# Block 0's routing moved into block 3's slots, with attention, table and load steps of a fused SSM and two-MoE kernel respaced

## The chip, the cores and the metric

One core of one Trainium2 chip runs the whole program. The metric is the device time of one execution in microseconds (us). The core has five engines with instruction queues of their own: TensorE (PE in the profile, with PEld for its weight loads), VectorE (DVE), ScalarE (ACT), GpSimd (POOL) and SyncE (SP, which here mainly issues DMA transfers). Each queue runs in order; engines wait for one another by semaphores.

## The reference

The program computes three layers one after the other.

```python
# 1: decayed linear attention: batch 4, heads 8, 768 steps, head size 32, state 16
y[:, :, sl] = einsum(C B * L, x) + einsum(C, state) * exp(cum)   # chunk by chunk, state carried on
x = y.transpose(0, 2, 1, 3).reshape(3072, 256)
# 2: an MoE layer without routing (leaky ReLU with a slope of its own for each feature)
h = x @ w_in                       # 256 -> 2048
x = (max(h, 0) + alpha * min(h, 0)) @ w_out     # 2048 -> 256
# 3: top-1 routing over 8 experts
logits = x @ w_gate + modality_bias[modality_id]
e = argmax(logits); gate = softmax(logits)[e]
out = gate * (max(x @ w1[e], 0) @ w2[e])        # 256 -> 1024 -> 256
```

## The kernel before

**Tiling.** The 3072 tokens are 24 chunks of 128. Chunks form nine blocks: blocks 0, 1 and 2 have two chunks, blocks 3 to 8 have three. A block goes through attention (`attn_*`, or `at_scan`, `at_mt`, `attn_c`, `attn_d` in the later part), then through layer 2 in 16 units of 128 features (`unit_mm` makes `ph`, `unit_act` and `unit_split` make `g`, `gh`, `gl`, `unit_g2` adds the second product into `px`), then through routing. Products are done in split precision: a high and a low part of each operand, three matmuls for one product.

**Two schedules.** Blocks 0 to 2 with the first attention stand in a part whose instruction order a scheduler chooses. From block 3 on the order is written by hand: a list of *slots*, 16 for each of the blocks 3 to 8 (slots 0 to 95, counted here from block 3's first unit), then 8 for each of 14 *items* (slots 96 to 207). An item is a page of up to 256 tokens of one expert in layer 3. A slot issues its unit's first product and activation, the split of the unit before, the second product of the unit four slots back (`LAG` is 4), and then whatever stands in the list `todo` for that slot, in the order in which the `do(...)` calls were made. Each engine runs its share of this in that order.

**Routing of a block k** (`route_at`): `route_mm` and `route_act` for each of its chunks (product `pxr`, logits `L`, and the copy of the tokens into the tile `xr` by ACT, line 499), `route_b` (which expert), `route_exp`, `route_gate` (the gate), `route_c` (product `pr`, counts in front of each token), `route_d` (row numbers `pi`), `route_out` (one indirect DMA by POOL per chunk, which scatters the rows of `xr` into the sorted DRAM array `srt`, line 573). For block 0 all of that stands ahead of the slots.

**Item tables.** When enough blocks have been counted, `item_tables` works out which expert and which page an item has: table 0 (items 0 and 1), table 1 (items 2 to 8), table 2 (the rest). It is a generator; each `yield` ends the step done in one slot. SP reads a table entry, then issues `item_load` (four transfers of 512 KB) and `item_rows` (258 KB out of `srt`). Each item's weights are split into high and low parts by ACT and DVE (`item_split`), its rows transposed (`item_tr_mm` on PE, `item_tr_act` on ACT and DVE, which give `x2h` and `x2l`). `tail_counts` writes zeros behind the last rows of every expert (eight writes of 645 KB).

**Shared buffers.** `ph`, and for blocks 0 to 2 `pxr` and `pr`, share three PSUM buffers (tag `h`). The attention's `ps` and `py` share two (tag `s`). `xr` has two SBUF buffers for all blocks in turn (`tag="xr"`, `bufs=2`), `xT` has one. `split_part` turns the attention's B and C into three bf16 parts each for chunks 17 to 23.

```python
    do(u, split_load, g)
    for q in range(6):
        do(v + q, split_part, g, q % 2, q // 2)
```

Of the kernel before, what the change touches and what calls it, by code (L numbers as in the profile page):

```python
# [35 lines left out]
NFULL = 12  # L36
# [76 lines left out]
def ssm_moe_moe_kernel(  # L113
# [25 lines left out]
    NS = 3  # L139
    blocks = [(sum(SIZES[:k]), n) for k, n in enumerate(SIZES)]  # L140
# [333 lines left out]
    def route_a(k, ts=None):  # L474

        n = blocks[k][1]
        for t in range(n) if ts is None else ts:
            route_mm(k, t)
            route_act(k, t)

    def route_mm(k, t):
        if t == 0:
            blk[k]["xr"] = work.tile([P, MX, ROW], F32, tag="xr", name="xr", bufs=2)
            blk[k]["L"] = small.tile([P, MX, NE], F32, tag="L", name="L")
        p = route_ps(k, [P, 512], "pxr", t)
        ts_ = slice(t * P, (t + 1) * P)
        pk = p[:, :KD * (P + NE)].rearrange("p (k w) -> p k w", k=KD)
        for kk in range(KD):
            mm(pk[:, kk], blk[k]["xT"][:, kk, ts_], idwg[:, kk], True, True)
        blk[k]["pk"] = pk  # L490
# [58 lines left out]
    def wait_for(i, o, why):  # L549
        tc.add_manual_dep(i, o.name, mybir.DependencyInfo(mybir.DependencyClass.Sync, mybir.DependencyReason.DATA),  # L550
                          reason=why)
# [18 lines left out]
    def route_out(k, ts):  # L570
        pi, xr = blk[k]["pi"], blk[k]["xr"]
        for t in ts:
            sc = nc.gpsimd.indirect_dma_start(
                out=srt[:, :], out_offset=bass.IndirectOffsetOnAxis(ap=pi[:, t:t + 1].bitcast(U32), axis=0),
                in_=xr[:, t, :ROW], in_offset=None, bounds_check=NROW - 1, oob_is_err=False)

            for o in scat + (tails if k < len(blocks) - 1 else []):
                tc.declare_no_dep(sc.ins, o, reason="rows are disjoint")
            scat.append(sc.ins)
            if k == len(blocks) - 1:  # L580
                for o in tails:
                    wait_for(sc.ins, o, "rows behind the last ones")
# [105 lines left out]
    def item_tables(j, pool):  # L688

        V = nc.vector
        use = cst[:, C_USE:C_E]
        u3 = use.rearrange("p (e j) -> p e j", j=NSL)
        cb = cnt[:, :, None].to_broadcast([P, NE, NSL])

        def compare(o, d, op):
            V.scalar_tensor_tensor(o.rearrange("p (e j) -> p e j", j=NSL), cb, d, u3, ALU.add, op)

        rk = pool.tile([P, 3, NS_], F32, tag="rk", name="rk", bufs=1)  # L700
        if j == 0:
            compare(sets[:, 0], -float(PG), ALU.is_ge)
            lo, hi, base = 0, 1, 0.0
        elif j == 1:
            compare(sets[:, 1], -float(PG), ALU.is_ge)
            compare(sets[:, 2], 0.0, ALU.is_gt)
            V.tensor_tensor(sets[:, 2], sets[:, 2], sets[:, 1], ALU.subtract)
            V.tensor_tensor(sets[:, 1], sets[:, 1], sets[:, 0], ALU.subtract)
            lo, hi, base = 0, 3, 0.0
        else:  # L710
            compare(sets[:, 0], -float(P), ALU.is_gt)
            compare(sets[:, 1], 0.0, ALU.is_gt)
            V.tensor_tensor(sets[:, 1], sets[:, 1], sets[:, 0], ALU.subtract)
            V.tensor_tensor(sets[:, :2], sets[:, :2], knw[:, None, :].to_broadcast([P, 2, NS_]), ALU.mult)
            lo, hi, base = 0, 2, float(N_KNOWN)
        w = hi - lo
        sf = sets[:, lo:hi].rearrange("p s n -> p (s n)")
        rf = rk[:, :w].rearrange("p s n -> p (s n)")
        V.tensor_tensor_scan(rf, cst[:, C_ONE:C_ONE + 1].to_broadcast([P, w * NS_]), sf, base, ALU.mult, ALU.add)
        yield  # L720
        if j == 2:

            nd = small.tile([P, 2], F32, tag="nd", name="nd", bufs=1)
            V.tensor_scalar(nd[:, 0:1], rk[:, 0, NS_ - 1:], float(-NFULL), 0.0, ALU.add, ALU.max)
            V.tensor_scalar(nd[:, 1:2], rk[:, 1, NS_ - 1:], float(-NSTATIC), 0.0, ALU.add, ALU.max)
            V.tensor_tensor(tbli, nd[:, 0:1], nd[:, 1:2], ALU.max)
            yield
        V.tensor_tensor(rf, rf, sf, ALU.mult)
        r1 = rk[:, 0]
        for s in range(1, w):  # L730
            V.tensor_tensor(r1, r1, rk[:, s], ALU.add)
        yield
        if j == 1:

            V.tensor_scalar(knw, r1, float(N_KNOWN), None, ALU.is_gt)
            nz = rk[:, 1]
            V.tensor_scalar(nz, r1, 0.0, None, ALU.is_equal)
            V.tensor_tensor(knw, knw, nz, ALU.add)
            yield
        va = pool.tile([P, 2, NS_], F32, tag="va", name="va", bufs=1)  # L740
        V.scalar_tensor_tensor(va, r1[:, None, :].to_broadcast([P, 2, NS_]), cst[:, C_IT:C_IT + 1],
                               cst[:, C_USE:C_IT].rearrange("p (r n) -> p r n", r=2), ALU.is_equal, ALU.mult)
        tf = small.tile([P, 2], F32, tag="tf", name="tf", bufs=1)
        V.tensor_reduce(tf, va, AX.X, ALU.add)
        V.tensor_copy(tab[j], tf)
        yield
# [169 lines left out]
    for u, (k, fc) in enumerate(early):  # L916
# [3 lines left out]
        if k == 0:  # L920
            g = fc // 2
# [17 lines left out]
        if side is not None:  # L939
# [5 lines left out]
            if left <= 0 or u + 1 == end:  # L945
# [1 line left out]
                    pass  # L947
                side = None
                nk += 1
    for step in (route_a, route_b, route_exp, route_gate, route_c, route_d):  # L950
        step(0)
    route_out(0, range(blocks[0][1]))

    last = len(blocks) - 1
    slots = [("m",) + q for q in late] + [("i", i, fc) for i in range(NSTATIC) for fc in range(KF2)]
    at = {q[1:]: u for u, q in reversed(list(enumerate(slots))) if q[0] == "m"}
# [4 lines left out]
    def do(u, fn, *args):  # L963
        todo.setdefault(u, []).append((fn, args))
# [65 lines left out]
    def route_at(k, mms, b):  # L1030
        for t, u in enumerate(mms):
            do(u, route_mm, k, t)
            do(u + 1, route_act, k, t)
        for v, fn in zip(b, (route_b, route_exp, route_gate, route_c, route_d)):
            do(v, fn, k)

        n = blocks[k][1]
        if k < last:
            for t in range(n):
                do(b[-1] + 1 + t, route_out, k, (t,))  # L1040
        else:
            do(b[-1], route_out, k, range(n))

    u = at[NS, 0]
    route_at(1, (u, u + 1), (u + 4, u + 5, u + 6, u + 7, u + 9))
    route_at(2, (u + 5, u + 7), (u + 9, u + 10, u + 11, u + 12, u + 15))
    for k in range(NS, last + 1):
        u = at[k, 15] + 1
        if k < last - 1:
# [4 lines left out]
    def table_at(u, j, pool):  # L1054
        steps = []

        def step():
            if not steps:
                steps.append(item_tables(j, pool[-1]))
            next(steps[0], None)  # L1060

        for v in range(u, u + 5):
            do(v, step)

    table_at(at[last - 1, 14], 0, small_)
    table_at(at[last, 13], 1, m2p)
    do(at[last, 11], tail_counts)
    table_at(ui + 12, 2, m2p)

    for k in range(NS, last):  # L1070
        c0, n = blocks[k + 1]
        if k == NS:
            do(at[k, 0], load_next, c0 + 1)
            do(at[k, 0], prep_dec, k + 1, 0)
        for j in range(n):
            c, b = c0 + j, at[k, 0] + 5 * j - (k > NS)
            for h in range(2):
                do(b + h, at_scan, c, h)
            do(b + 2, at_mt, c, k + 1, j)
            do(b + 2, load_next, c + 2)  # L1080
            if j + 1 < n:
                do(b + 3, prep_dec, k + 1, j + 1)
            do(b + 4, attn_c, c, k + 1, j)
            do(b + 5, attn_d, c, k + 1, j)
        if k + 2 <= last:
            do(at[k, 9], load_block, k + 2)
            do(at[k, 15], prep_dec, k + 2, 0)
    for g, u, v in ((1, at[NS, 8], at[NS + 1, 1]),):
        do(u, split_load, g)
        for q in range(6):  # L1090
            do(v + q, split_part, g, q % 2, q // 2)
    do(at[NS, 15], new_pools)
    do(at[last - 1, 15], end_attention)

# [1 line left out]
    do(at[last, 3], item_rows, 0)  # L1096
    do(at[last, 4], lambda: item_load(1))
    do(at[last, 4], item_rows, 1)
    do(at[last, 13], item_tr_mm, 0)
    do(at[last, 14], item_tr_act, 0)  # L1100
    do(ui + 2, item_tr_mm, 1)
    do(ui + 3, item_tr_act, 1)
    for q in range(8):
# [1 line left out]
        do(at[last, 15] + q, item_split, 1, q // 2, (q % 2,))  # L1105
    for i in range(2, NSTATIC):
        b = ui + KF2 * (i - 2)
        do(b, item_load, i, 1 if i >= NFULL else 2)
        do(b if i == 2 else b + 6, item_rows, i)
        b += KF2  # L1110
        for q in range(8):
            do(b + q, item_split, i, q // 2, (q % 2,))
        do(b + 4, item_tr_mm, i)
        do(b + 5, item_tr_act, i)

# [101 lines left out]
```

## Time and profile before

| | us |
|---|---|
| median of 3 runs | 583.43 |
| lowest and highest | 581.81, 584.33 |
| the profiled execution | 582.98 |
| its span, first to last instruction | 581.2 |
| TensorE busy in the span | 552.0 |
| DVE, ACT, POOL busy | 434.1, 315.0, 238.9 |

The span is 1.8 us shorter than that execution's own time, which also holds what lies before the first and behind the last instruction. Slot 0 begins at 145.7 us in the profile, slot 16 (block 4) at 192.6, slot 96 (item 0) at 401.3; the last product ends near 567.

### The profile page before, as it was taken

What the parts mean: (1) busy time and instruction counts of PE and PEld (TensorE: products, weight loads), DVE (VectorE), ACT (ScalarE), POOL (GpSimd) and SP (SyncE); (2) the same over time, 40 slices, a digit from 0 to 9 for tenths busy, and PEclk for the clock granted to TensorE, in tenths of its full rate; (3) what the DMA queues carried; (4) which work ended last, traced back from release to release, by engine and by line L of the source; (5) the groups of instructions that cost most, each with busy time, mean ns of one, the idle gap of its engine ahead of it and who ended that gap; (6) DMA issues with size and microseconds to landing.
All of it is one profiled execution on the core that took longest, in us unless ns stands there. A gap on an engine that the chain in (4) does not pass through costs nothing. (4 is left out here: it accounts for less than half of the span.)

```text
span 581.2 us, 12122 instructions
## 1 busy us (share of the span) xinstructions
PE 552.0 (95%) x4303; PEld 516.9 (89%) x4303; DVE 434.1 (75%) x857; ACT 315.0 (54%) x696; POOL 238.9 (41%) x258
## 2 busy tenths in 40 slices
PE   8989989998999989999999999997999999999993
PEld 7867878898989779999998999997999999999993
DVE  4999999834677777777767776579688778777860
ACT  0446657756434464444443444575567776677761
POOL 1144345655445645654754844746022122111211
PEclk9795999999799999999999999999999999999998
DMA  7956654420037245234234210468969867776400
GB/s 240 296 179 199 191 186 130 148 77 12 19 109 209 81 131 173 88 107 150 68 114 147 79 46 2 146 210 226 284 227 327 254 212 225 235 240 202 152 17 6
DMA packets 59123, 89.27 MB, mean 154 GB/s; under 512 B 5070, under 2 KB 37008, under 8 KB 59056
## 3 DMA queue, kind: packets, MB, share of 16 engines
q1 hardware_dynamic: 55942, 80.73, 44.7%
q0 software_dynamic: 2400, 6.32, 3.0%
q10 hardware_dynamic: 714, 1.38, 0.8%
q8 instruction: 36, 0.59, 0.4%
q14 instruction: 31, 0.25, 0.1%
HBM read 73.50 MB, written 15.17 MB: 153 GB/s over the span
## 5 line engine op out<-in xcount | busy, mean ns | idle before, releaser
L622 POOL TENSOR_TENSOR gl<-g,gh 128x384 fp32r<-128x384 f32 (+1 forms) x144 | 143.0, 994 | 147.6 <-ACT gh L620 147.1
L611 ACT ACTIVATE t<-ph,sgn 128x384 f32<-128x384 f32 (+1 forms) x144 | 78.6, 546 | 121.8 <-PE ph L153 115.2
L613 DVE SCALAR_TENSOR_TENSOR g<-ph,sal,t 128x384 f32<-128x384 f32 (+1 forms) x144 | 81.2, 565 | 76.4 <-ACT t L611 69.7
L153 PE MATMUL ph<-xh,wi_h 128*128 128x384 f32 (+1 forms) x288 | 99.3, 347 | 2.7 <-DVE g L613 2.4
L153 PE MATMUL px<-gl,wo_h 128*128 128x384 f32 (+1 forms) x288 | 94.2, 327 | 2.3 <-POOL gl L622 2.2
L153 PE MATMUL px<-gh,wo_h 128*128 128x384 f32 (+1 forms) x288 | 93.7, 326 | 0.2 <-ACT xT L650 0.2
L153 PE MATMUL ph<-xl,wi_h 128*128 128x384 f32 (+1 forms) x288 | 92.8, 323 | 1.1 <-DVE xl L159 1.1
L153 PE MATMUL px<-gh,wo_l 128*128 128x384 f32 (+1 forms) x288 | 93.3, 324 | 0.4 <-DVE wo_l L159 0.4
L153 PE MATMUL ph<-xh,wi_l 128*128 128x384 f32 (+1 forms) x288 | 92.8, 323 | 0.0
L620 ACT CAST gh<-g 128x384 fp32r<-128x384 f32 (+1 forms) x144 | 67.6, 470 | 17.1 <-DVE g L613 16.5
L880 POOL DMA_INDIRECT out_dram<-ob,xr x26 | 29.3, 1126 | 112.0 <-ACT ob L879 55.4
L857 ACT ACTIVATE rh<-ph 128x256 fp32r<-128x256 f32 (+1 forms) x112 | 41.6, 371 | 53.0 <-PE ph L153 51.4
L153 PEld LDWEIGHTS ph<-xh,wi_h 128*128 128x128 f32 x288 | 55.1, 192 | 7.9 <-DVE g L613 3.9
L858 DVE SCALAR_TENSOR_TENSOR rl<-ph,rh 128x256 fp32r<-128x256 f32 (+1 forms) x112 | 45.1, 402 | 21.4 <-ACT rh L857 20.4
L153 PEld LDWEIGHTS px<-gl,wo_h 128*128 128x128 f32 x288 | 55.7, 193 | 4.0 <-POOL gl L622 2.7
L153 PEld LDWEIGHTS ph<-xl,wi_h 128*128 128x128 f32 x288 | 55.3, 192 | 1.6 <-DVE xl L159 1.4
L153 PEld LDWEIGHTS px<-gh,wo_h 128*128 128x128 f32 x288 | 55.8, 194 | 1.0 <-ACT xT L650 0.5
L153 PEld LDWEIGHTS px<-gh,wo_l 128*128 128x128 f32 x288 | 55.8, 194 | 0.8 <-DVE wo_l L159 0.6
L153 PEld LDWEIGHTS ph<-xh,wi_l 128*128 128x128 f32 x288 | 55.3, 192 | 0.2 <-issue 0.2
L969 DVE TENSOR_TENSOR_SCAN ab<-ab,id 128x512 f32<-128x512 f32 x30 | 44.0, 1468 | 0.0
L153 PE MATMUL ph<-x2h,wi_h 128*128 128x256 f32 x144 | 41.3, 286 | 0.0
L153 PE MATMUL ph<-x2l,wi_h 128*128 128x256 f32 x144 | 40.4, 280 | 0.0
(149 smaller groups left out, 1291.0 us busy)
## 6 DMA issues: line engine op xcount, KB each, us to landing
raw<-in_w_dram SPq DMA_DIRECT2D x56, 512.0 KB
ab<-a_scr SPq DMA_DIRECT2D x24, 512.0 KB
srt<-zr SPq DMA_DIRECT2D x8, 645.0 KB
raw<-in_w_in_dram SPq DMA_DIRECT2D x8, 512.0 KB
raw<-in_w_out_dram SPq DMA_DIRECT2D x8, 512.0 KB
xr<-srt SPq DMA_DIRECT2D x14, 258.0 KB
bs<-bcs SPq DMA_DIRECT2D x30, 96.0 KB
bs<-bcs SPq DMA_DIRECT2D x15, 192.0 KB
```

Source lines behind the costliest of these rows:

```text
L153: nc.tensor.matmul(o, l, r, start=start, stop=stop)
L611: nc.scalar.activation(t[:, :N], ph[:, :N], AF.Copy, scale=sg)
L613: nc.vector.scalar_tensor_tensor(g[:, :N], ph[:, :N], sal[:, fc:fc + 1], t[:, :N], ALU.mult, ALU.max)
L620: nc.scalar.copy(gh[:, :N], g[:, :N])
L622: nc.gpsimd.tensor_tensor(gl[:, :N], g[:, :N], f(gh[:, :N]), ALU.subtract)
L857: nc.scalar.activation(rh[:, :n], ph[:, :n], AF.Relu)
L858: nc.vector.scalar_tensor_tensor(rl[:, :n], ph[:, :n], 0.0, f(rh[:, :n]), ALU.max, ALU.subtract)
L880: nc.gpsimd.indirect_dma_start(out=out[:, :], out_offset=bass.IndirectOffsetOnAxis(ap=xr[:, t, ROW - 1:ROW].bitcast(U32), axis=0), in_=ob, ...
L969: nc.vector.tensor_tensor_scan(lt[:, s_].rearrange("p h i -> p (h i)"), lt[:, s_].rearrange("p h i -> p (h i)"), id8[:, s_].rearrange("p h ...
```

## The change

- Ahead of the slots only `route_a(0)` is left. Block 0's `route_b`, `route_exp`, `route_gate`, `route_c`, `route_d` go to slots 0 to 4, its two scatters to slots 5 and 6.
- Block 2's `route_d` goes from slot 15 to slot 13, its scatters from 16 and 17 to 14 and 15.
- In block 3's slots the attention of chunks 10 and 11 begins one slot sooner (slots 4 and 9).
- The six `split_part` steps stand in every second slot (17, 19, ... 27) and no more in six slots running.
- Table 1 has two more steps, so that its last one is in slot 98 and no more in 96; item 2's load, and with it its rows and its splits, come two slots later (98 and 106 to 113). Item 0's transposes come one slot sooner (92, 93) and are registered ahead of the table's steps.

```diff
         elif j == 1:
             compare(sets[:, 1], -float(PG), ALU.is_ge)
             compare(sets[:, 2], 0.0, ALU.is_gt)
+            yield
             V.tensor_tensor(sets[:, 2], sets[:, 2], sets[:, 1], ALU.subtract)
             V.tensor_tensor(sets[:, 1], sets[:, 1], sets[:, 0], ALU.subtract)
             lo, hi, base = 0, 3, 0.0
...
+        if j == 1:
+            yield
         w = hi - lo
...
-    for step in (route_a, route_b, route_exp, route_gate, route_c, route_d):
-        step(0)
-    route_out(0, range(blocks[0][1]))
+    route_a(0)
...
     u = at[NS, 0]
+    route_at(0, (), (u, u + 1, u + 2, u + 3, u + 4))
     route_at(1, (u, u + 1), (u + 4, u + 5, u + 6, u + 7, u + 9))
-    route_at(2, (u + 5, u + 7), (u + 9, u + 10, u + 11, u + 12, u + 15))
+    route_at(2, (u + 5, u + 7), (u + 9, u + 10, u + 11, u + 12, u + 13))
...
-        for v in range(u, u + 5):
+        for v in range(u, u + 7):
             do(v, step)
 
+    do(at[last, 12], item_tr_mm, 0)
+    do(at[last, 13], item_tr_act, 0)
     table_at(at[last - 1, 14], 0, small_)
     table_at(at[last, 13], 1, m2p)
...
-            c, b = c0 + j, at[k, 0] + 5 * j - (k > NS)
+            c, b = c0 + j, at[k, 0] + 5 * j - (k > NS or j > 0)
...
-            do(v + q, split_part, g, q % 2, q // 2)
+            do(v + 2 * q, split_part, g, q % 2, q // 2)
...
-    do(at[last, 13], item_tr_mm, 0)
-    do(at[last, 14], item_tr_act, 0)
...
-        do(b, item_load, i, 1 if i >= NFULL else 2)
-        do(b if i == 2 else b + 6, item_rows, i)
+
+        w = 2 if i == 2 else 0
+        do(b + w, item_load, i, 1 if i >= NFULL else 2)
+        do(b + w if i == 2 else b + 6, item_rows, i)
         b += KF2
         for q in range(8):
-            do(b + q, item_split, i, q // 2, (q % 2,))
+            do(b + w + q, item_split, i, q // 2, (q % 2,))
```

## Rows read from the trace of the kernel before

**Rows 1.** The page's first part: busy time, share of the span, instructions.

```profile
PE 552.0 (95%) x4303; PEld 516.9 (89%) x4303; DVE 434.1 (75%) x857; ACT 315.0 (54%) x696; POOL 238.9 (41%) x258
```

**Rows 2.** Stages: length, busy us (instructions) by engine, granted clock, DMA share, GB/s.

```profile
143.40:161.70 18.30, 15.64 (x105) 14.49 (x104) 12.73 (x38) 7.52 (x19) 8.38 (x10) 0.81 0.13 41
...
405.80:409.30 3.50, 3.50 (x16) 3.50 (x15) 3.40 (x8) 1.34 (x4) 1.01 (x1) 0.52 1.09 271
412.30:430.00 17.70, 17.32 (x151) 17.08 (x150) 12.50 (x41) 11.39 (x28) 1.00 (x1) 1.00 1.02 303
432.50:567.00 134.50, 134.45 (x1145) 134.25 (x1144) 104.87 (x206) 94.22 (x218) 27.33 (x25) 1.00 0.65 203
```

**Rows 3.** TensorE's timeline, slots 0 to 5: start, us, line, [idle before <-releaser].

```profile
142.28 1.09 PE L153 MATMUL pxr<-idwg,xT 128*128 128x136 f32 x8
...
145.55 0.17 PE L153 MATMUL pr<-oh,tri 128*128 128x8 bf16 x1 [2.18 <-DVE oh L519]
...
146.73 0.52 PE L153 MATMUL ph<-xh,wi_l 128*128 128x384 f32 x1
...
153.39 0.28 PE L153 MATMUL px<-gh,wo_l 128*128 128x256 f32 x1
...
161.75 0.45 PE L153 MATMUL ph<-xh,wi_h 128*128 128x384 f32 x1
...
164.41 0.39 PE L153 MATMUL ps<-bs 128*128 128x128 bf16 x4
```

**Rows 4.** TensorE's timeline in block 4's slots: rows with a wait.

```profile
194.16 0.44 PE L153 MATMUL ph<-xl,wi_h 128*128 128x384 f32 x1 [1.13 <-DVE xl L159]
...
213.67 0.50 PE L153 MATMUL pxr<-idwg,xT 128*128 128x136 f32 x2 [1.22 <-ACT xr L499]
...
217.34 0.61 PE L153 MATMUL pxr<-idwg,xT 128*128 128x136 f32 x3 [0.85 <-DVE mt L983]
```

**Rows 5.** The timeline of VectorE and TensorE where item 0 begins.

```profile
397.33 1.76 DVE L698 SCALAR_TENSOR_TENSOR sets<-cnt,cst 128x96 f32<-128x96 f32 x2
...
404.40 0.68 DVE L841 TENSOR_TENSOR x2l<-pt,x2h 128x512 fp32r<-128x512 f32 x1
...
405.14 0.38 PE L153 MATMUL ph<-x2l,w1h 128*128 128x256 f32 x1 [3.55 <-DVE x2l L841]
```

**Rows 6.** VectorE's timeline: the first and the last of block 0's 13 routing instructions.

```profile
143.98 0.17 DVE L509 TENSOR_REDUCE mx<-L 128x2 f32<-128x16 f32 x1
...
146.55 0.17 DVE L567 CAST pi<-pf 128x2 int32<-128x2 f32 x1
```

**Rows 7.** VectorE's timeline in slot 5: the last step of `attn_d`.

```profile
165.16 0.42 DVE L159 TENSOR_TENSOR xl<-py,xh 128x256 fp32r<-128x256 f32 x1 [0.44 <-ACT xh L325]
```

**Rows 8.** DMA issues in 178:186, 255:300 and 390:402: scatters, count, us to landing.

```profile
srt<-xr,pi POOLq DMA_INDIRECT x2, 5.3
...
srt<-xr,pi POOLq DMA_INDIRECT x3, 3.4
...
srt<-xr,pi POOLq DMA_INDIRECT x3, 6.8
```

**Rows 9.** TensorE's timeline around an earlier idle time, in block 0.

```profile
43.14 0.39 PE L153 MATMUL px<-gl,wo_h 128*128 128x256 f32 x1 [2.17 <-POOL gl L622]
...
57.40 0.41 PE L153 MATMUL ph<-xh,wi_l 128*128 128x256 f32 x1
```

**Rows 10.** SP's queue from the zero writes to item 2's rows.

```profile
394.70 12.83 SPq L461 DMA_DIRECT2D srt<-zr  x8
409.84 4.27 SPq L787 DMA_DIRECT2D raw<-in_w_dram  x4
418.82 0.38 SPq L794 DMA_DIRECT2D xr<-srt  x1
```

**Rows 11.** ScalarE's timeline: the first split of item 2's weights, in slot 104.

```profile
424.21 0.63 ACT L819 CAST wi_h<-raw 128x512 fp32r<-128x512 f32 x1
```

**Rows 12.** TensorE's timeline: item 2's transposes, in slot 108.

```profile
429.21 0.60 PE L831 MATMUL pt<-cst,xr 128*128 128x128 f32 x4
```

## The prediction

> **What bounds the kernel now.** I read the page's busy shares first, then stretches of time by stage, then TensorE's waits, then the timelines around the three places that the diff touches. TensorE is busy 552.0 of 581.2 us [rows 1]; 29 us are left in all, so only a place where it stands idle or runs at half its clock can give time back. From 432.5 to 567 it is busy 134.45 of 134.50 us [rows 2]: a microsecond won ahead of 432 reaches the end whole, as long as the item loads keep up.
>
> The idle time that this diff touches lies in three places. Ahead of block 3, TensorE has finished block 0's `pxr` at 143.4 (142.28 + 1.09) and waits 2.18 us for the first `pr`, because VectorE works through `route_b`; the products behind it then run at half speed, 0.52 us where the clock is 1.2 GHz, until 153.4 [rows 3]. In block 4's slots it waits 1.13, 1.22 and 0.85 us for results that stand late in VectorE's and ScalarE's queues [rows 4]. At item 0 it waits 3.55 us for `x2l`, which stands on VectorE behind the table's steps that begin at 397.33 [rows 5], and runs at half speed for 3.5 us more, 0.52 granted in 405.8 to 409.3 [rows 2].
>
> **Part 1: block 0's routing moves.** The 13 VectorE instructions from 143.98 to 146.7 [rows 6] are not removed; they go behind `g` of slots 0 to 4. TensorE loses no product either. Two bounds for the gain. TensorE's own: the idle 2.18 us and half of the slow stretch, 146.7 to 153.4 [rows 3], make 2.18 + 3.35 = 5.5 us. VectorE's: it was busy 12.73 of the 18.30 us from 143.4 to slot 5 [rows 2, 3], and it keeps all that work, so slot 5 can't come more than 5.6 us sooner. Lower bound: the idle 2.18 us alone. Walking both queues through slots 0 to 4 with the old durations, VectorE is seldom free and TensorE waits for it twice, by 0.8 and 0.4 us. I take 3.8 (2.2 to 5.5).
>
> **Part 2: chunk 10 one slot sooner.** `attn_d` of chunk 9 and the second `ps` of chunk 10 now both stand in slot 5. The two PSUM buffers of that tag are then held by `py` and the first `ps`, so TensorE must wait until `xl` has read `py`. Before, `xl` began 3.4 us after the slot's first product (161.75, 165.16) and took 0.42 [rows 3, 7]; the `ps` of that slot stood 2.7 us behind the same product (164.41). That is a wait of 1.1 us, 1.5 with `route_d`, `route_b` and a scan now ahead of it. I take a loss of 1.5 (0.5 to 2.2). For chunk 11 the same spacing as before moves as a whole: 0.
>
> **Part 3: the buffers of `xr`.** The tile has two buffers. Block 2 takes the one of block 0, first written by ScalarE's copy in slot 6. Before, block 0's scatters were issued ahead of slot 5, a whole routing earlier. Now the second scatter of block 0 is issued in the same slot 6, on POOL behind a `gl`, and the copy may begin only when that DMA has read its rows and reported. No run of before has such a wait, so it is bounded by the time from issue to landing of these scatters: 3.4 us in a quiet stretch, 5.3 and 6.8 in busy ones [rows 8]. ScalarE stands still meanwhile, and queued behind the copy are `t` of slot 7 and all later activations; `pxr` of block 2's second chunk needs the PSUM buffer that this copy frees, so TensorE stops in slot 7. POOL's scatter comes about 0.1 us after the copy would be ready, TensorE reaches its `pxr` about 0.8 us later, and the copy itself adds 0.4: the idle time is the landing less 0.3 us, 3.1 to 6.5. Chunk 11's and 12's loads move at that time, less than in the busiest rows; between 3.4 and 5.3 I take 4.4, so 4.1 us.
>
> The Trainium skill (DMA: Bandwidth & Descriptors, "Anatomy of one DMA — SWDGE (gpsimd) path") gives a DMA issued by GpSimd about 2.0 us plus its bytes over 436 GB/s; for 132 KB that is an estimate of 2.3 us, and the sum would be about 2.1 us smaller, more if the clock then held. The shortest row, 3.4 us, doesn't agree, and the sum goes by the rows.
>
> An idle time of 2.17 us and one of 3.55 us were each followed by half speed [rows 5, 9]. The stretches were 3.5 us, 6.7 us, and some 14 us after 43.14, where the 256-column product at 57.40 still takes 0.41 us and not 0.28 [rows 2, 3, 9]. Half of the stretch is lost: 1.75, 3.35 or 7. I take 2.5, between the first two, since in slots 8 and 9 no second long idle time follows soon. While TensorE is late, VectorE catches up, which saves a wait of 0.4 us in slot 8. Part 3 costs 4.1 + 2.5 - 0.4 = 6.2 us (2 to 13).
>
> **Part 4: slots 14 to 27.** `attn_d` of chunk 11 comes a slot ahead of block 4's first unit, and block 2's `route_d` no longer stands in front of it. The wait of 1.13 us at 194.16 [rows 4] and the thinner issue around it (the slot began at 192.58) go: 1.7 us. The six parts, each a conversion on ScalarE and a transfer whose issue also holds that queue, stand in every second slot; four also have a subtraction on VectorE. The waits of 1.22 and 0.85 us [rows 4] were behind them; in the slots between both engines can now catch up. I take 1.8 of 2.1 (0.5 to 2.1), since slots 21 and 23 take two of the subtractions. Block 2's scatters one slot pair sooner cost nothing: POOL is idle half of 143.4 to 161.7 [rows 2] and no more loaded here.
>
> **Part 5: table 1 and item 0.** `x2l` is now queued in slot 93, ahead of the table's first step at 397.33 [rows 5]. It is done near 398.2 and item 0 needs it at 401.3, so the 3.55 us go, and with them half of 3.5 us at the low clock: 5.3 us together. The table's VectorE work is the same, spread over slots 93 to 98 in pieces of at most 2 us, and `g` comes between them. What is late next: VectorE still lags through slots 96 to 99, `x2l` of item 1 is done about 1 us after TensorE asks for its buffer for block 8's `pxr`, which takes 0.7 back. VectorE was busy 12.50 of 17.70 us in 412.3 to 430 [rows 2] and can catch up. I take 4.6 (1.6 to 5.3).
>
> Item 2's load is issued when the table is done: near 409 by VectorE's queue, as before (409.84 [rows 10]), while TensorE is 5.3 us further. Its first split was at 424.21 [rows 11] and comes 5.3 us sooner and two slots of 1.4 us later (97 item slots in the 134.5 us to 567), near 421.7. The zero writes ahead of it, eight of 645 KB issued from 394.70 and landed by 418.82 when the rows' load behind them went out [rows 10], and its own 2.1 MB at the 303 GB/s of that stretch [rows 2] put its first quarter near 417 and its last near 422. That is hidden, with little to spare. The rows, issued at 418.82, are needed by the transposes at 429.21 [rows 12] less 5.3, near 424: 5 us, enough but only just.
>
> **Sum.** 3.8 - 1.5 - 6.2 + 1.7 + 1.8 + 4.6 = 4.2 us gained. The profiled execution took 582.98 us (span 581.2 and 1.8 around it), which gives 578.8; the median of the runs is 0.45 us above that execution, so I predict 579.2.
>
> **Rivals.**
>
> *The `xr` wait is short or not there.* If a scatter reports after 2.3 us or so, or the copy finds a free buffer, TensorE idles 0 to 2 us in slot 7 and the clock stays: the 6.2 us of part 3 become 0 to 2, the time 573 to 575, say 574. For it: block 0's and block 1's scatters never held anything before. Against: two buffers, three blocks, and 3.4 us as the shortest row. Chance 0.24.
>
> *The item loads take part 5 back.* DMA is full from 395 to 428 (share 1.02 in 412 to 430 [rows 2]) and doesn't get faster because TensorE does. If item 2's rows or first weights land 3 us later than worked out, ScalarE or TensorE waits for them and 1.6 of 4.6 us stay: 582.2, no change that can be told. Against: 5 us in hand for both. Chance 0.14.
>
> *The low clock after the `xr` wait lasts as long as after 43.14.* Then 7 us are lost and not 2.5, and with a landing of 6.8 us (2.4 more) part 3 costs 13.1: 579.2 + 6.9 = 586.1, slower. It decides from a stretch of some 10 us at half speed on. For it: that is what one of three idle times did. Against: the two others were much shorter. Chance 0.08.
>
> **Chances and range.** The forecast has 0.54, with a range of its own of 576 to 582. About 0.5% (2.9 us) is what a measurement of this kernel can tell from no change, so faster means below 580.5: 0.39 of the forecast's 0.54, the first rival's 0.24 and 0.03 of the second, 0.66. Slower, above 586.3, is half of the third, 0.05 with what I have not thought of. The rest, 0.29, is the same. The range goes from the first rival to the second, 573 to 583, and leaves out the third and the edges of the others.
>
> **What would show it.** Part 1: no wait for `oh` near 143 and a full clock in 144 to 154. Part 2: TensorE waiting about 1.5 us for `xl` in slot 5. Part 3, the step on which most hangs: ScalarE's copy of block 2's first chunk into `xr` waiting 3 to 6 us with a DMA as releaser, and TensorE idle about 4 us in slot 7, half speed behind it. If that is absent, the time is near 574. Part 4: no wait for `xl` at slot 16, ScalarE waits shorter in slots 20 to 23. Part 5: no wait for `x2l` at item 0 and a full clock behind it; a wait of PE for item 2's rows or of ScalarE for its raw weights would show the second rival.

## The result, and the profile after

The changed kernel takes 577.98 us (median of 20 runs, 576.61 to 583.93), the kernel before 584.03 us (20 runs, 579.94 to 586.66): a ratio of 0.9911, 95% interval 0.9897 to 0.9926. It is 0.9% faster, where 579.2 was predicted.

The page's first part, of the changed kernel: busy time, share of the span, instructions. TensorE's products are as many as in [rows 1]; about half of the 5.2 us less of busy time is fewer of them at the low clock (the mean granted clock was 0.967 over 581.2 us and is 0.971 over 576.1), the rest is not placed.

```profile
span 576.1 us, 12113 instructions
PE 546.8 (95%) x4303; PEld 513.1 (89%) x4303; DVE 432.2 (75%) x857; ACT 314.4 (55%) x696; POOL 239.3 (42%) x258
```

Stages of the changed kernel (length; busy us and instructions of PE, PEld, DVE, ACT, POOL; granted clock, DMA share, GB/s):

```profile
143.40:161.70 18.30, 16.90 (x130) 15.14 (x128) 15.40 (x43) 8.66 (x23) 7.67 (x10) 1.00 0.12 43
161.70:190.00 28.30, 23.06 (x157) 20.96 (x156) 18.17 (x42) 9.36 (x21) 15.44 (x16) 0.94 0.48 133
395.00:408.00 13.00, 13.00 (x87) 12.96 (x86) 12.48 (x28) 8.79 (x20) 6.88 (x6) 1.00 1.08 277
428.00:562.00 134.00, 134.00 (x1144) 134.00 (x1143) 104.66 (x203) 94.13 (x219) 27.48 (x25) 1.00 0.66 206
```

The first stretch, at 0.81 in [rows 2], now has the full clock and no wait for `oh`; TensorE is busy in every microsecond from 395 to 408, where it waited 3.55 us for `x2l` [rows 5]. The loss is in the second line. TensorE's timeline there and at item 2's transposes, the rows with a wait and two at the low clock:

```profile
162.77 0.40 PE L153 MATMUL ps<-bs 128*128 128x128 bf16 x4 [1.07 <-DVE xl L159]
...
169.98 0.73 PE L153 MATMUL pxr<-idwg,xT 128*128 128x136 f32 x4 [2.47 <-ACT xr L499]
171.19 0.69 PE L153 MATMUL ph<-xh,wi_h 128*128 128x384 f32 x1 [0.47 <-DVE g L613]
171.67 0.52 PE L153 MATMUL ph<-xl,wi_h 128*128 128x384 f32 x1
...
173.91 0.52 PE L153 MATMUL px<-gl,wo_h 128*128 128x384 f32 x1
...
182.68 0.40 PE L153 MATMUL ps<-bs 128*128 128x128 bf16 x4 [1.23 <-DVE xl L159]
...
424.43 0.63 PE L834 MATMUL pt<-cst,xr 128*128 128x128 f32 x4 [1.91 <-DMA xr<-srt]
```

Who held the 2.47 us, on the timelines of POOL and ScalarE: block 0's second scatter is issued at 166.59, and the copy into the buffer that it reads starts 2.97 us later, released by that DMA.

```profile
166.59 1.01 POOL L573 DMA_INDIRECT srt<-xr,pi  x1 [0.15 <-DVE sm L533]
...
169.56 0.37 ACT L499 COPY xr<-pxr 128x256 f32<-128x256 f32 x1 [4.21 <-DMA srt<-xr,pi]
```

Who held the 1.91 us, in SyncE's queue: the zero writes, item 2's four weights, and, 24.8 us after the first zero write, the load of item 2's rows; 6.4 us later TensorE has them.

```profile
393.24 13.56 SPq L461 DMA_DIRECT2D srt<-zr  x8
408.21 5.55 SPq L790 DMA_DIRECT2D raw<-in_w_dram  x4
418.06 0.38 SPq L797 DMA_DIRECT2D xr<-srt  x1
```

To add up the parts I set the two traces against each other at the first product of a slot, counted from block 0's first `pxr` (142.28 before, 142.82 after), since the stretch ahead of it varies from execution to execution. The changed kernel is ahead by 4.5 us at slot 2, 3.4 at slot 5, -2.3 at slot 16, 1.9 at slot 24, 7.4 at slot 98 and 5.6 from slot 113 to the last.

### The profile page after: what moved, and what is told of

Read it like the earlier page. It is cut to its first block, busy times and chain, and to the rows that moved or that the text cites. A ratio compares the mean times of both kernels' runs of the same rounds, so it can differ in the third digit from the quotient of the medians.

```text
span 576.1 us, 12113 instructions
## 1 busy us (share of the span) xinstructions
PE 546.8 (95%) x4303; PEld 513.1 (89%) x4303; DVE 432.2 (75%) x857; ACT 314.4 (55%) x696; POOL 239.3 (42%) x258
## 5 line engine op out<-in xcount | busy, mean ns | idle before, releaser
L622 POOL TENSOR_TENSOR gl<-g,gh 128x384 fp32r<-128x384 f32 (+1 forms) x144 | 145.5, 1012 | 140.6 <-ACT gh L620 138.8
```

What stands on the lines that cost most here:

```text
L622: nc.gpsimd.tensor_tensor(gl[:, :N], g[:, :N], f(gh[:, :N]), ALU.subtract)
```

## The experiments

Ratios are to runs of the kernel before, taken beside each group of runs on the same chip, with 95% intervals. "Ahead" is the time won by a slot, counted as above.

**First: the two waits, and parts 1 and 5 alone.**

Block 0's `xr` in a buffer of its own:

```diff
-            blk[k]["xr"] = work.tile([P, MX, ROW], F32, tag="xr", name="xr", bufs=2)
+            n = blocks[k][1]
+            if k == 0:
+                blk[k]["xr"] = work.tile([P, n, ROW], F32, tag="xr0", name="xr0", bufs=1)
+            else:
+                blk[k]["xr"] = work.tile([P, MX, ROW], F32, tag="xr", name="xr", bufs=2)
```

> The changed kernel with one edit: block 0's `xr` lies in a buffer of its own (two chunks wide), so block 2 takes a buffer that nobody has used. Theory (part 3, the buffer): the profile of the changed kernel has ACT 4.21 us idle before block 2's copy at 169.56, PE 2.47 us idle before 169.98 and 0.47 before 171.19, and products of 0.52 us instead of 0.26 until 174.53, about 1.5 us more; all of it goes, 4.4 us, and the time is about 573.6 (572.5 to 575). First rival (the work that part 1 put into slots 0 to 6 is itself late on VectorE or ScalarE, and the buffer only ended the wait last): another releaser takes over and less than 1.5 us is won, 576.5 or more. Second rival (the low clock comes of the crowded slots and not of the idle time): the idle 2.9 us goes, the 0.52-us products stay, about 575.1.

Measured: 577.45 against 583.84, ratio 0.9914 (0.9885 to 0.9944): not told apart from the changed kernel. The first rival's time, but not its reason. The wait is gone and so is the low clock behind it. Ahead at slot 24: 5.86 us where the changed kernel has 1.94, so the shared buffer cost 3.9 us, where the theory had 4.4. They last until slot 108 (11.7 against 7.4) and are then lost at item 2's rows, in TensorE's timeline and SyncE's queue of this kernel:

```profile
388.88 13.54 SPq L461 DMA_DIRECT2D srt<-zr  x8
404.08 6.40 SPq L794 DMA_DIRECT2D raw<-in_w_dram  x4
415.34 0.38 SPq L801 DMA_DIRECT2D xr<-srt  x1
```

```profile
421.46 1.09 PE L838 MATMUL pt<-cst,xr 128*128 128x128 f32 x4 [3.39 <-DMA xr<-srt]
...
423.20 0.41 PE L153 MATMUL ph<-x2l,wi_h 128*128 128x256 f32 x1
```

The window behind that wait has a granted clock of 0.51. Wait and low clock take 5.8 us of 11.7.

Item 2's transposes a slot later:

```diff
-        do(b + 4, item_tr_mm, i)
-        do(b + 5, item_tr_act, i)
+        o = 5 if i == 2 else 4
+        do(b + o, item_tr_mm, i)
+        do(b + o + 1, item_tr_act, i)
```

> The changed kernel with one edit: the transposes of item 2's rows and the casts behind them come one slot later (item slots 5 and 6 of item 1 in place of 4 and 5). Theory (part 5, the rows of item 2 land late because their load was moved two slots back): PE's 1.91 us before the transposes at 424.43 shrinks by one item slot, about 1.4 us, and nothing else waits, since the item's first product is two slots behind; about 576.6 (576 to 577.2). Rival (ScalarE or VectorE have no time one slot later, so the casts come after item 2's first product wants them): a wait of 0.5 to 1.5 us before that product instead, 577.5 to 578.5.

Measured: 579.79, ratio 0.9938 (0.9913 to 0.9963): a miss for the theory and for the rival. TensorE waits 2.09 us at the transposes all the same, because the rows were there 32.8 us after the first zero write (426.31 - 393.52) and not 31.2, and the clock behind that wait is 0.74 from 425 to 430. From slot 108 to 113 it loses 3.5 us (7.5 to 4.0), the changed kernel 1.8. Why the rows came later is open.

Part 1 alone on the kernel before:

```diff
-    for step in (route_a, route_b, route_exp, route_gate, route_c, route_d):
-        step(0)
-    route_out(0, range(blocks[0][1]))
+    route_a(0)
...
+    route_at(0, (), (u, u + 1, u + 2, u + 3, u + 4))
```

> The kernel before with part 1 alone: block 0's routing in slots 0 to 6, everything else as before (chunk 10's attention, block 2's `route_d`, the parts, the tables and the item loads at their old places). Theory: slots 0 to 5 win 3.4 us as in the changed kernel, and the wait of block 2's copy for block 0's scatter takes 4.4 back, so about 585 against 584 of before (583.5 to 586.5), with ACT idle about 4 us before a copy into `xr` near 169 and products of 0.52 us after it. Rival (the loss from slot 6 on comes of chunk 10's attention a slot sooner, part 2, that this kernel does not have): 3.4 us faster, about 580.6.

Measured: 584.53 against 583.84, ratio 1.0023 (1.0002 to 1.0044). The theory holds, the rival (part 2 as the cause of the loss) falls. Ahead by 4.5 us at slot 2, 3.6 at slot 7, 0.1 at slot 10. The copy that waits is the same one:

```profile
169.22 0.37 ACT L499 COPY xr<-pxr 128x256 f32<-128x256 f32 x1 [4.19 <-DMA srt<-xr,pi]
```

Part 5 alone on the kernel before:

```diff
+            yield
...
-        for v in range(u, u + 5):
+        for v in range(u, u + 7):
...
+    do(at[last, 12], item_tr_mm, 0)
+    do(at[last, 13], item_tr_act, 0)
...
-        do(b, item_load, i, 1 if i >= NFULL else 2)
+        w = 2 if i == 2 else 0
+        do(b + w, item_load, i, 1 if i >= NFULL else 2)
```

> The kernel before with part 5 alone: table 1 in seven steps, item 0's transposes and casts a slot sooner, item 2's load and splits two slots later. Theory: independent of block 3's slots; PE's 3.55 us before 405.14 goes with the half clock behind it (5.3), and item 2's rows, now late, take 1.9 back, so about 3.4 us faster, 580.6 (579.5 to 581.5). Rival (the gain there was only possible because work came earlier in block 3's slots): under 2 us, 582 or more.

Measured: 583.86 against 583.84, ratio 0.9997 (0.9973 to 1.002). A miss for the theory's size: ahead by 5.4 us at slot 98, as worked out, and by -1.3 at slot 113. The loss is 6.7 and not 1.9, at the same place, and the zero writes are 34.2 us old when the rows are there:

```profile
395.84 15.42 SPq L461 DMA_DIRECT2D srt<-zr  x8
412.10 7.78 SPq L790 DMA_DIRECT2D raw<-in_w_dram  x4
423.65 0.38 SPq L797 DMA_DIRECT2D xr<-srt  x1
```

```profile
430.00 1.09 PE L834 MATMUL pt<-cst,xr 128*128 128x128 f32 x4 [4.88 <-DMA xr<-srt]
```

One of its twelve runs took 578.2 us, the others 582.5 and more.

**Second: is it the order of the loads, and what is part 4 worth?** The edit for the first three: in `item_load`, behind the reading of the expert's number, item 2's rows are loaded ahead of its weights.

```diff
+        if i == 2:
+            item_rows(i)
         pool = rawp if i % 2 == 0 else m2p[0]
...
-        do(b + w if i == 2 else b + 6, item_rows, i)
+        if i > 2:
+            do(b + 6, item_rows, i)
```

> The changed kernel with one edit: SyncE issues the load of item 2's rows ahead of the four loads of its weights instead of behind them. Theory (the rows are late because their load waits until the zero rows that are written behind the known ones have landed, and that is held up by 2 MB of weights that share the DMA engines): the zero writes (issued from 393.24, landed before 418.06 in the changed kernel) are done by about 415, the rows land by about 419, the 1.91 us at 424.43 goes, and the weights, now later, are still there before the splits want them in order; 576.1 (575.3 to 577). Rival (the zero writes alone fill the DMA engines and the weights now come behind them): the first splits wait for weights, item 2's first product waits for its weights and the time is 578 or more.

Measured: 581.38 against 583.10, ratio 0.9971 (0.9949 to 0.9994), slower than the changed kernel; the rival holds. The rows' load, which waits for the zero writes, goes out 26.6 us after the first of them, no sooner than in the changed kernel (24.8). The DMA engines then stand nearly still, as the weights wait behind that load, and ScalarE's first split waits 5.08 us for them. Windows, SyncE's queue and the split:

```profile
395.00:417.00 22.00, 21.62 (x156) 21.38 (x155) 19.11 (x41) 13.55 (x30) 7.88 (x7) 1.00 1.06 245
419.00:421.00 2.00, 2.00 (x25) 1.96 (x24) 1.23 (x6) 0.39 (x1) 0.00 (x0) 1.00 0.09 28
```

```profile
394.38 15.01 SPq L461 DMA_DIRECT2D srt<-zr  x8
421.01 0.40 SPq L799 DMA_DIRECT2D xr<-srt  x1
421.62 6.80 SPq L792 DMA_DIRECT2D raw<-in_w_dram  x8
```

```profile
425.36 0.62 ACT L824 CAST wi_h<-raw 128x512 fp32r<-128x512 f32 x1 [5.08 <-DMA raw<-in_w_dram]
```

TensorE's 1.91 us at the transposes becomes 0.36, and waits of 1.04, 0.95 and 1.07 us for VectorE and ScalarE, which do the splits late, come in the slots behind.

> Both edits on the changed kernel: block 0's `xr` in a buffer of its own, and item 2's rows loaded ahead of its weights. Theory: in the first of the two alone, 4.1 us were won by 211 and 4.45 by 405, and 3.5 of them were lost again at item 2's rows (3.39 us of wait and a half clock after it); without that wait the 4.4 us and the 1.9 of the wait both show, 578.0 - 4.4 - 1.9 = 571.7 (571 to 573). Rival (the end is set by the DMA engines from the zero writes on, whatever the order): 576 or more.

Measured: 577.09, ratio 0.9895 (0.9858 to 0.9931): the rival's time; in the trace it lies between the two. The rows' load goes out 24.9 us after the first zero write, against 26.5 in the kernel with the buffer alone. Ahead by 11.4 us at slot 108 and by 8.7 at slot 113; the wait for rows is gone, the late splits take 2.8. That is 3.1 more than the changed kernel keeps, but the stretch ahead of block 3, which no edit touches, was 2.6 us longer in this execution (`pxr` at 145.43 and not 142.82), and whether that goes with the kernel or with the execution can't be told.

> The kernel before with part 5 and item 2's rows loaded ahead of its weights. Part 5 alone measured as before (583.86 against 583.84), with PE 4.88 us idle at item 2's transposes and the clock at 0.75 in that stretch. Theory (part 5 wins its 5.3 us at item 0 in any case and loses them at item 2's rows): with the rows in time it is 5.3 us faster, about 578.6 (577.8 to 580). Rival (what part 5 wins at item 0 is lost at item 2's weights if not at its rows): 582 or more.

Measured: 580.86, ratio 0.9973 (0.9948 to 0.9997), between the two. Ahead by 5.4 us at slot 98, all of it kept to slot 108, and 3.0 from slot 113 on, after waits of 0.98 and 1.07 us in the slots of the late splits. The rows' load goes out 24.4 us after the first zero write, where it was 27.8 with part 5 alone.

Part 4 alone on the kernel before:

```diff
-    route_at(2, (u + 5, u + 7), (u + 9, u + 10, u + 11, u + 12, u + 15))
+    route_at(2, (u + 5, u + 7), (u + 9, u + 10, u + 11, u + 12, u + 13))
...
-            do(v + q, split_part, g, q % 2, q // 2)
+            do(v + 2 * q, split_part, g, q % 2, q // 2)
```

> The kernel before with part 4 alone: block 2's `route_d` two slots sooner and the parts in every second slot. Theory: 1.7 and 1.8 us by the terms of the sum, 3.5 us faster, 580.3 (579.5 to 581.5); PE's waits of 1.13 at 194.16, 1.22 at 213.67 and 0.85 at 217.34 are gone. Rival (those waits went in the changed kernel because everything in front of them had been moved, and alone part 4 gives the parts' copies to slots that have other work on ScalarE): under 1.5 us, 582.3 or more.

Measured: 579.01 against 583.10, ratio 0.9924 (0.9898 to 0.995): alone as fast, within the intervals, as the whole change (0.9911, 0.9897 to 0.9926). The waits of [rows 4] are gone. It is 4.0 us ahead at slot 24, 1.1 of them at slot 17; 0.8 go again at item 0, where the wait for `x2l` remains and the low clock beside it lasts 7 us, from 400.4 to 407.4 (granted 0.51).

**Third: the bytes.** If the DMA engines set the time at which item 2's rows are there, fewer bytes must move it.

```diff
-TAIL = 5 * P
+TAIL = 4 * P
```

> The changed kernel with block 0's `xr` in a buffer of its own, and with 4 in place of 5 x 128 zero rows written behind each expert's known rows (4.1 MB in place of 5.2; it leaves out part of the zeroing that the kernel does for any routing). Theory (from the zero writes on the 16 DMA engines are busy without a break at some 250 GB/s until item 2's rows are in, and that sets when its transposes can run): 1 MB less brings the rows 4.2 us sooner; the kernel with the buffer alone waited 3.39 us and ran at half clock after it, 5 to 6 us in all; about 572 (571 to 573.5). Rival (the rows wait for a table, or for the order on SyncE, and not for bytes): 576.5 or more.

Measured: 573.07 against 584.52, ratio 0.9828 (0.98 to 0.9857). The theory. The rows' load goes out 22.0 us after the first zero write, and TensorE no longer waits:

```profile
390.08 12.31 SPq L461 DMA_DIRECT2D srt<-zr  x8
405.29 2.27 SPq L794 DMA_DIRECT2D raw<-in_w_dram  x4
412.12 0.38 SPq L801 DMA_DIRECT2D xr<-srt  x1
```

```profile
419.11 0.60 PE L838 MATMUL pt<-cst,xr 128*128 128x128 f32 x4
```

Ahead by 11.7 us at slot 108 and 11.7 at slot 113: nothing is given back.

> The kernel before with 4 in place of 5 x 128 zero rows behind each expert's known rows, and nothing else (a control; it leaves out the same part of the zeroing). Theory: item 2's rows came before TensorE wanted them, so 1 MB less wins nothing: 583.5 (582.5 to 584.5). Rival (the busy DMA engines also hold up something on the path at item 0, where TensorE waits 3.55 us): 1 us faster or more, 582 or less.

Measured: 583.81 against 584.52, ratio 0.999 (0.9979 to 1.0002). The theory: by itself the smaller write brings nothing that can be told.

> The kernel before with part 5 and 4 in place of 5 x 128 zero rows. Theory: part 5 alone won 5.4 us at item 0 and lost 6.7 at item 2's rows (4.88 us of wait and a clock of 0.75 in that stretch); with the rows 4.2 us sooner some 0.7 of the wait is left: 578.5 to 580. Rival as in the first: 582 or more.

Measured: 577.36 against 584.52, ratio 0.9883 (0.9863 to 0.9903), better than expected: no wait at the transposes, ahead by 5.4 us at slot 98 and by 5.5 at the end.

The last one differs from the first of this group by one line:

```diff
-            c, b = c0 + j, at[k, 0] + 5 * j - (k > NS or j > 0)
+            c, b = c0 + j, at[k, 0] + 5 * j - (k > NS)
```

> The first of these with chunk 10's attention back at its old slots (without part 2). Theory: part 2 costs the 1.25 us that TensorE waits for `xl` before chunk 10's products of `bs`, and part 4 does without it (alone, it has no wait in these slots and won 4.1 us there): 0.6 to 1.2 us faster than the first, about 571. Rival (part 2 makes room for the parts and for block 2's routing): the waits of the kernel before come back at block 4's slots and it is as long as the first or longer, 572 or more.

Measured: 571.71 against 584.52, ratio 0.9777 (0.976 to 0.9793), the fastest kernel here; the theory. Ahead by 7.5 us at slot 24 where the first has 5.9: part 2 costs 1.6. At the last slot 1.2 of them are left, after a wait of 0.55 us at item 2's rows. The waits for `xl` (1.07 and 1.26 us there) are gone. As it leaves out part of the zeroing, it shows what the other parts are worth and is no replacement; of the kernels that do all the work none was told apart from the changed one as faster.

## Why the prediction was right, and where it was not

The time was 1.2 us off, and that is partly luck: the gain was 1.9 off. 4.2 us were worked out, and the medians are 6.05 apart; the kernel before took 0.6 us more in these runs than in those that the prediction started from. Two terms of the sum were off by more than the others, and in opposite directions: part 3 was priced 2.3 us too dear, part 5 net 1.0 too good.

| term | predicted | measured | from |
|---|---|---|---|
| part 1 | +3.8 | +3.6 | part 1 alone, slot 7 |
| part 2 | -1.5 | -1.6 | with and without it, slot 24 |
| part 3 | -6.2 | -3.9 | with and without the buffer, slot 24 |
| part 4 | +1.7 + 1.8 | +4.0 | part 4 alone, slot 24 |
| part 5 | +4.6 | +5.4 at item 0, -1.8 at item 2's rows | changed kernel, slots 98, 113 |

The column of measured terms makes 5.7, and the trace of the changed kernel is 5.6 us ahead.

*Part 1* was right in mechanism and size. But 2.6 of its 3.6 us are the low clock that followed the wait for `oh` in the profile of before: an execution of the kernel with smaller zero writes has the same wait and no low clock (last section), and measured from that one part 1 would be worth some 1.0 us, less than the lower bound of 2.2.

*Part 2* was right: the wait for `xl` in slot 5 is there (1.07 us), and a second one of 1.23 came in slot 10, where I had said 0.

*Part 3* was right as a mechanism: the copy, the DMA as releaser, TensorE stopping in slot 7, the half clock behind it. The term that was mis-sized is the landing, 4.4 us taken and 2.97 measured, and with it the idle time: 2.47 + 0.47 us, not 4.1. In the four executions that show this wait the copy starts 2.7 to 3.0 us after the scatter's issue. The 0.52-us products go from 171.67 to 174.2, some 2.9 us with the first slow one; half of that, 1.4, is lost and not 2.5. Without the wait TensorE would have stood 0.58 us for `g` in that slot (the kernel with the buffer does), close to the 0.4 that the sum takes off; 2.9 + 1.4 - 0.6 makes 3.7 of the 3.9. The scatter was faster than the shortest row that I had (3.4 us [rows 8]). The Trainium skill (DMA: Bandwidth & Descriptors, "Anatomy of one DMA — SWDGE (gpsimd) path") gives an estimate of 2.3 us for it; the measured 2.97 doesn't agree, and lies nearly midway between that and the shortest row. The rival without the wait was wrong, and the rival with a long low clock too.

*Part 4* was right, 0.5 us larger than worked out.

*Part 5* failed in one step: "5 us, enough but only just" for item 2's rows. I gave the load 5 us to land and had no row for how long it takes behind 2 MB of weights in the same queue. No wait in the trace of before shows it, but its packets do: the last of that load's 256 packets of 1032 bytes ends 5.66 us after the issue at 418.82, and where TensorE waited for these rows with the weights ahead of them, it began 0.6 to 0.7 us after the last packet. That makes 6.3 us (6.4 in the changed kernel), so the rows are there near 425.1, behind the 424 that the text names. With the rows ahead of the weights the load took 3.0 us (421.01 to 424.00). The 0.7 us that the text takes back for item 1's `x2l` did not show: TensorE waits 0.38 us for it in either kernel. The loss in the changed kernel, 1.8 us, is thus the second rival in small. On the kernel before, part 5 alone meets that rival in full.

What this step hid is the main finding: from the zero writes on, another resource keeps the time. In the changed kernel the DMA share is 1.09 at 270 GB/s while the zeros go out, with the first of the weights, and 1.06 at 365 GB/s while the rest of the weights and the rows do:

```profile
395.00:417.00 22.00, 21.62 (x159) 21.38 (x158) 18.56 (x44) 13.78 (x31) 6.88 (x6) 1.00 1.09 270
417.00:424.00 7.00, 5.52 (x54) 5.28 (x52) 5.55 (x25) 4.21 (x11) 0.00 (x0) 1.00 1.06 365
```

Eight zero writes of 645 KB, 2.1 MB of weights and the rows must pass. TensorE's distance from the first zero write to the transposes was 429.21 - 394.70 = 34.5 us before [rows 10, 12], and the rows needed 24.1 to the issue of their load and 6.3 from there, 30.4. Part 5 takes its 5.3 us out of that distance: 29.2 are left, 30.6 with the transposes a slot later. What the rows needed in each profiled execution, less that distance, is the wait:

| kernel | rows there after the first zero write | left over the distance | TensorE waited |
|---|---|---|---|
| changed | 424.43 - 393.24 = 31.2 | 2.0 | 1.91 |
| buffer | 421.46 - 388.88 = 32.6 | 3.4 | 3.39 |
| transposes later | 426.31 - 393.52 = 32.8 | 2.2 | 2.09 |
| part 5 alone | 430.00 - 395.84 = 34.2 | 5.0 | 4.88 |
| 1 MB less, without part 2 | 418.88 - 389.18 = 29.7 | 0.5 | 0.55 |

The lines behind the third and the fifth row, SyncE's queue and TensorE's timeline of each kernel:

```profile
393.52 13.35 SPq L461 DMA_DIRECT2D srt<-zr  x8
...
426.31 0.63 PE L834 MATMUL pt<-cst,xr 128*128 128x128 f32 x4 [2.09 <-DMA xr<-srt]
...
389.18 12.28 SPq L461 DMA_DIRECT2D srt<-zr  x8
...
418.88 0.63 PE L838 MATMUL pt<-cst,xr 128*128 128x128 f32 x4 [0.55 <-DMA xr<-srt]
```

That is why part 5 wins nothing alone, and 5.5 us in the trace with 1 MB less. It is also where the buffer's 3.9 us went: they move the zero writes too and should have come through, but in that kernel the rows needed 1.4 us more, and the longer wait was followed by a clock of 0.51; with 1 MB less both are gone, 573.07 (ratio 0.9828) against 577.45 (0.9914). Why the same bytes take 31 us in one kernel and 34 in another stays open. The difference lies ahead of the rows' load, in the zero writes: with the weights behind them the load went out 24.1 to 28.4 us after the first one, with the rows ahead of the weights 24.4 to 26.6, so whether the weights hold the zeros up is not shown either way.

## What to carry to other kernels

A chain on another resource that runs beside the one you speed up has a length of its own: measure it from its first issue to its consumer, the last transfer's own landing included, and compare it with the distance that is left after the change; what is won between its start and its consumer beyond that margin is lost. Before moving a step past others, count the buffers of its tile and ask when the last reader of each, a DMA too, reports. And time the parts alone: here part 4 gave as much as all together, part 1 lost its gain again through a buffer that two blocks share, and part 5 was worth nothing until 1 MB of zero writes was gone.

## What the runs showed of the hardware

An idle TensorE was not always followed by the low clock. In the kernel with smaller zero writes alone, the same waits as in [rows 3] and [rows 5] were followed by full speed:

```profile
149.92 0.17 PE L153 MATMUL pr<-oh,tri 128*128 128x8 bf16 x1 [2.17 <-DVE oh L519]
...
150.30 0.34 PE L153 MATMUL ph<-xl,wi_h 128*128 128x384 f32 x1
...
406.87 0.38 PE L153 MATMUL ph<-x2l,w1h 128*128 128x256 f32 x1 [3.55 <-DVE x2l L841]
407.09 0.28 PE L153 MATMUL ph<-x2h,w1l 128*128 128x256 f32 x1
```

That execution is 2.6 us ahead of the one of before at slot 2 and 4.2 at slot 98, with an edit that touches neither place. Of the six executions with the wait for `oh` (2.17 to 2.18 us), five have some 7 us at the low clock behind it and this one has none; of the four with the wait for `x2l` at item 0 (3.55 to 3.58 us), two have some 3.5 us at the low clock, one 7 and this one none. At item 2's rows the changed kernel's wait of 1.91 us has the full clock behind it (1.00 from 424.4 to 430), the one of 2.09 us with the transposes later 0.74. So a single profiled execution doesn't say what the low clock behind a wait costs; what decides it, no run here shows. The stretch ahead of block 3, which no edit touches, took from 142.0 to 146.7 us in the 14 profiled executions, a spread larger than every part of this change but part 5's 5.4 us at item 0.

With the DMA engines full, 245 GB/s went through while the zero writes did (the kernel with the rows first, where none of item 2's weights stand among them) and 365 while the weights did. The Trainium skill (DMA: Bandwidth & Descriptors, "Specifications") gives some 358 GB/s per core as the limit of the memory. The weights' stretch lies 2% above that, and the zeros stay some 30% below it; no run here shows why.
